# Attention block inputs in one 256 KB transfer, zero-padded V in the first batch, and a new table of ranks

## The chip, the core and the metric

The kernel runs on one core of a Trainium2 chip. The metric is the device time of one execution in microseconds (us); the kernel before has a median of 495.89 us over 3 runs. The engines are TensorE (PE, with its weight loads as PEld), VectorE (DVE), ScalarE (ACT), GpSimd (POOL) and SyncE (SP), which here only issues DMA transfers.

## The reference

Four batches, 8 heads, 768 tokens, 64 numbers a head. Each token attends to the first 8 tokens (global) and to itself and the 95 before it (local), with a distance bias per head. A gated MLP over the tokens follows.

```python
scores = q @ k.T / sqrt(64) - slope[h] * dist      # kept where global or local
a = softmax(scores)
x = (a @ v), heads side by side                    # [4, 768, 512]
h = relu(x @ w_in); u, v2 = h[..., :512], h[..., 512:]
vn = (v2 - mean(v2)) / sqrt(var(v2) + 1e-6)
out = (u * (w_spatial @ vn + b_spatial)) @ w_out   # w_spatial mixes the 768 tokens
```

## The kernel before

A batch is six blocks of 128 tokens, so there are 24 blocks, n = 0 to 23. For a block, `prep` (line 856) and `prep_v` (line 904) load q, k and v, `scores` (line 935) makes the probabilities and `values` (line 1003) multiplies them with V. A block's keys are its own 128 tokens and the 128 before it, whose first 32 rows are overwritten with the batch's global tokens; the block that opens a batch has its own 128 alone. So a block has 1 or 2 chunks of 128 keys.

The first batch (blocks 0 to 5) works in plain float32 (`whole_s`, `whole_v`), where a matrix product is two rows of the profile. From block 6 on, every operand is split into a high part `hi` and the rest `lo` (`hi_lo`, line 641), and the products are made of the parts. For that `prep` loads a block's q and k into `raw`, splits them (`split_qk`, line 887), and copies the parts by DMA into the layouts `q1`, `ql` and `kring` (`prep_k`, line 897): 18 transfers a block in all.

In `values` the probabilities of a pair of heads are transposed on PE, copied by ACT from a PSUM bank to `pth`, and multiplied with V into `ops`. In the first batch one product per pair and chunk multiplies 128 columns of V (two heads) with 256 columns of probabilities (both heads' tokens). Half of the result is wanted: head 0's rows under head 0's tokens and head 1's under head 1's. So two ACT copies of 64 rows each bring the halves together in a tile `c`, and from `c` the parts `xth` and `xtl` of x are made:

```python
ops[:, g % 2] = vring[:, chunk, g*128:(g+1)*128].T @ pth[:, chunk]   # [128, 256]
xs[0:64]   <- ops[0:64, :, 0:128]       # ACT, tile c
xs[64:128] <- ops[64:128, :, 128:256]   # ACT, tile c
xh <- xs ; xl <- xs - xh                # any engine
```

Meanwhile the weights are prepared. `w_in` and `w_out` arrive as 64-bit floats, in pieces of 512 KB into three `u` buffers, and `split_weights` (line 723) turns each into `hi` and `lo` with some ten instructions on DVE, ACT and POOL. The eight pieces of `w_in` end with eight DVE writes of `w_in_l`: the first four belong to the V half of the MLP (`mlp_v`, 128x512 products), the last four to the U half (`mlp_u`, products of `xth` and `xtl` with `w_in`, 128x256). `w_t` is the spatial matrix.

The order is not that of the code. All instructions are recorded, and `plan` (line 347) sorts them for all engines at once by a model of costs, with a rank for each step from the table `KEYS` (line 533). `keep_warm` then puts products with the identity matrix (`bank<-ident`), which nobody reads, into gaps that the plan foresees on PE. SP runs its list in order: a transfer that waits holds all behind it.

Of the kernel before, what the change touches and what calls it, by code (L numbers as in the profile page):

```python
# [10 lines left out]
F32 = mybir.dt.float32  # L11
# [15 lines left out]
CFG = {'WS': 6, 'WV': 6, 'kept': 'p', 'bias1': 'pppppppp', 'bias2': 'a', 'S': [['I01', 'A'], ['I00', 'T00', 'T01', 'A', 'V00', 'B00'], ['T02', 'T03', 'A', 'V01', 'U00'], ['T04', 'T05', 'A', 'V02'], ['Q00', 'Q01', 'A', 'V03', 'U01'], ['Q02', 'Q03', 'A', 'V04']], 'T': [['V15', 'U12', 'A'], ['G10', 'O10', 'A'], ['G11', 'O11', 'A'], ['G12', 'O12', 'V00', 'V01', 'U00', 'A'], ['V02', 'A'], ['V03', 'U01', 'A', 'V04']], 'END': ['V05', 'U02', 'G00', 'O00', 'G01', 'O01', 'G02', 'O02'], 'whi': 'aaax', 'wsub': 'xx', 'wadd': 'v', 'wth': 'a', 'wtl': 'p', 'vhi': 'p', 'vlo': 'p', 'qhi': 'xv', 'qlo': 'v', 'khi': 'a', 'klo': 'v', 'pth0': 'a', 'x0h': 'a', 'x0l': 'v', 'pth': 'a', 'xh': 'aa', 'c1': 'a', 'xl': 'vppv', 'vnh': 'xvpa', 'vnl': 'p', 'gm': 'x', 'gh': 'aa', 'gl': 'x', 'o': 'vava', 'norm0': 'p', 'norm': 'p', 'wp': 3, 'we': 'p', 'x0c': 1, 'xch': 'x', 'xcl': 'x', 'vrn': 'v', 'dup': 1, 'fold': '', 'xb': 1, 'div': 'v', 'rows': 'a', 'xf0h': 'aa', 'xf0l': 'pppp', 'xdiv': 'v', 'xbh': 'a', 'xbl': 'p', 'b_rawqk': 1, 'b_ev': 3, 'b_raw': 1, 'b_pr': 10, 'b_pth': 2, 'b_c1': 3, 'b_ps_s': 2, 'b_ps_p': 2, 'b_ps_o': 2, 'b_ps_m': 2}  # L27
# [195 lines left out]
def cost(op):  # L223

    out = op.writes[0]
    n = elements(out)
    src = op.reads[0] if op.reads else out
    psum = any(in_psum(x) for x in op.reads + op.writes[:1])
    parts = list(out.ap)[0][1]
    if op.eng == "tensor":  # L230
        if op.call == "transpose":
            return 109, 0, False
        n = elements(op.kw["rhs"])
        if op.kw["rhs"].dtype == F32:
            return 4 * max(n, 128) * .422, 0, False
        return {128: 111, 256: 120, 512: 229}[n], 0, False
    if op.eng == "sync":
        return 650, 330 + n * 4 * parts * .0024, False
# [298 lines left out]
def attn_then_spatial_gating_kernel(  # L537
# [23 lines left out]
    def cp(e, out, in_):  # L561
# [21 lines left out]

    B, NB, D, H, _ = q.shape
# [66 lines left out]

    def even(t):
        return t.rearrange("p (g two) x -> p two g x", two=2)[:, 0]

    def odd(t):
        return t.rearrange("p (g two) x -> p two g x", two=2)[:, 1]
# [66 lines left out]
    def split_weights(src, hi, lo, tag, x):  # L723
# [10 lines left out]
        if CFG["wp"] == 3:  # L734
# [7 lines left out]
            nc.vector.tensor_scalar(out=c, in0=m, scalar1=UPPER_MAX, scalar2=UPPER_MIN, op0=ALU.min, op1=ALU.max)  # L742
            nc.vector.tensor_scalar(out=ci, in0=ci, scalar1=4, scalar2=1, op0=ALU.logical_shift_left, op1=ALU.logical_shift_right)
            nc.vector.scalar_tensor_tensor(out=ci, in0=ci, scalar=0x40000000, in1=ai, op0=ALU.bitwise_xor, op1=ALU.bitwise_or)
            nc.vector.tensor_scalar(out=ai, in0=ci, scalar1=-0x800000, scalar2=None, op0=ALU.bitwise_and)
# [110 lines left out]
    def prep(n):  # L856
        b, i = divmod(n, NB)
        if whole_s(n):
            if n == 0:
                for x in range(2):  # L860
                    t = ring["q", x] = work.tile([P, H, P], F32, name="q0", tag=f"q{x}", bufs=1)
                    nc.gpsimd.memset(even(t)[64:128], 0.0)
                    nc.gpsimd.memset(odd(t)[0:64], 0.0)
# [503 lines left out]
```

## Time and profile before

| what | value |
|---|---|
| median of 3 runs | 495.89 us (495.59 to 496.63) |
| the profiled execution | 494.69 us |
| its span, first to last instruction | 492.9 us |
| PE busy | 472.0 us (96%), 3240 instructions |
| DVE, ACT, POOL busy | 357.2, 292.7, 273.0 us (72%, 59%, 55%) |
| mean busy share of the 16 DMA engines, queue q1 | 50.0% |
| mean granted TensorE clock | 0.994 |

The three times are those of the runs, the span is of one of them under the profiler; 1.8 us of that execution lie outside the span. PE's rows overlap, since a product starts before the one ahead has left the array: how long one takes is read from start to start in a dense stretch. Tile names stand without buffer numbers; `bank` is a PSUM bank, `ev` and `u` are scratch tiles of several uses.

### The profile page before, as it was taken

What the parts mean: (1) busy time and instruction counts of PE and PEld (TensorE: products, weight loads), DVE (VectorE), ACT (ScalarE), POOL (GpSimd) and SP (SyncE); (2) the same over time, 40 slices, a digit from 0 to 9 for tenths busy, and PEclk for the clock granted to TensorE, in tenths of its full rate; (3) what the DMA queues carried; (4) which work ended last, traced back from release to release, by engine and by line L of the source; (5) the groups of instructions that cost most, each with busy time, mean ns of one, the idle gap of its engine ahead of it and who ended that gap; (6) DMA issues with size and microseconds to landing.
All of it is one profiled execution on the core that took longest, in us unless ns stands there. A gap on an engine that the chain in (4) does not pass through costs nothing.

```text
span 492.9 us, 9972 instructions
## 1 busy us (share of the span) xinstructions
PE 472.0 (96%) x3240; PEld 430.8 (87%) x3240; DVE 357.2 (72%) x1014; ACT 292.7 (59%) x793; POOL 273.0 (55%) x429
## 2 busy tenths in 40 slices
PE   7988899999999999999999999999999999999995
PEld 7866597899999889898989999999988989999994
DVE  5789958785889788888868788787757598561532
ACT  3799789844754777676556566766733586520111
POOL 3689987777435564697565354794342565452000
PEclk9999999999999999999999999999998999999999
DMA  7995326237655767555573663766552671000012
GB/s 178 267 226 180 107 82 187 70 97 178 154 155 149 204 171 202 149 135 134 155 198 93 180 167 98 184 155 173 123 139 76 159 177 56 16 0 3 23 43 72
DMA packets 68269, 65.51 MB, mean 133 GB/s; under 512 B 6672, under 2 KB 49936, under 8 KB 68208
## 3 DMA queue, kind: packets, MB, share of 16 engines
q1 hardware_dynamic: 68208, 64.78, 50.0%
q8 instruction: 28, 0.46, 0.4%
q14 instruction: 33, 0.27, 0.2%
HBM read 29.76 MB, written 6.68 MB: 74 GB/s over the span
## 4 chain that ended last, share of the span: by engine, by line
PE 73%; ACT 7%; DMA 6%; DVE 4%; POOL 4%; SPq 3%; issue 2%; ACTq 0%; POOLq 0%
PE bank L39 64%; PE ops L39 8%; SPq L39 3%; ACT pr L39 3%; DMA raw<-in_k_dram 2%; DMA kring<-raw 2%; DVE bank L39 1%; POOL pr L39 1%; ACT ev L39 1%; DMA vring<-vg 1%; DMA q<-raw 1%; ACT pth L39 1%; ACT w_in_h L39 1%; ACT c L39 1%; POOL vring L39 1%
## 5 line engine op out<-in xcount | busy, mean ns | idle before, releaser
L39 POOL TENSOR_SCALAR pr<-pr,rc 128x256 f32<-128x256 f32 (+1 forms) x192 | 95.3, 513 | 41.7 <-DVE rc L39 24.8
L39 ACT ACTIVATE pr<-pr,mn 128x256 f32<-128x256 f32 (+1 forms) x192 | 92.0, 482 | 15.6 <-DVE mn L39 14.9
L39 DVE CUSTOM_DVE_ANT_0 pr<-bank,bias 128x256 f32<-128x256 f32 (+1 forms) x192 | 68.1, 396 | 19.0 <-PE bank L39 18.3
L39 DVE TENSOR_TENSOR c<-ops,c 64x256 f32<-64x256 f32 x144 | 60.5, 420 | 16.3 <-ACT c L39 13.0
L39 ACT ACTIVATE pth<-bank 128x512 fp32r<-128x512 f32 (+3 forms) x96 | 52.4, 558 | 31.1 <-PE bank L39 19.5
L39 PE MATMUL ops<-pth,vring 128*128 128x256 f32 x352 | 66.1, 313 | 4.3 <-ACT pth L39 1.7
L39 PE MATMUL bank<-kring,q 128*128 128x256 f32 (+1 forms) x384 | 66.9, 304 | 3.1 <-DVE w_in_l L39 1.4
L39 PE MATMUL bank<-ident,pr 128*128 128x128 f32 x352 | 60.6, 273 | 1.9 <-ACT pth L39 1.4
L39 PEld LDWEIGHTS ops<-pth,vring 128*128 128x128 f32 x352 | 51.8, 189 | 11.3 <-ACT c L39 3.5
L39 PEld LDWEIGHTS bank<-kring,q 128*128 128x128 f32 x384 | 55.0, 189 | 7.3 <-DVE w_in_l L39 1.8
L39 POOL TENSOR_TENSOR xtl<-c,xth 128x256 fp32r<-128x256 f32 x44 | 32.8, 747 | 50.7 <-ACT xth L39 47.3
L39 DVE TENSOR_TENSOR pth<-bank,pth 128x512 fp32r<-128x512 f32 (+1 forms) x72 | 45.5, 642 | 13.0 <-ACT pth L39 12.0
L39 PEld LDWEIGHTS bank<-ident,pr 128*128 128x128 f32 x352 | 43.3, 140 | 9.8 <-POOL pr L39 2.4
L39 PE MATMUL bank<-w_t_h,vnh 128*128 128x256 f32 x288 | 45.6, 285 | 1.1 <-ACT vnh L39 1.1
L39 PE MATMUL bank<-w_t_h,vnl 128*128 128x256 f32 x288 | 45.4, 284 | 0.0
L39 PE MATMUL bank<-w_t_l,vnh 128*128 128x256 f32 x288 | 45.0, 283 | 0.0
L39 ACT ACTIVATE c<-ops 64x256 f32<-64x256 f32 x96 | 36.3, 378 | 14.3 <-PE ops L39 12.2
L39 ACT ACTIVATE ev<-bank 128x512 f32<-128x512 f32 (+1 forms) x37 | 21.5, 585 | 37.1 <-PE bank L39 31.0
L39 PEld LDWEIGHTS bank<-w_t_h,vnh 128*128 128x128 f32 x288 | 38.6, 189 | 1.4 <-ACT vnh L39 1.3
L39 PEld LDWEIGHTS bank<-w_t_h,vnl 128*128 128x128 f32 x288 | 38.9, 189 | 0.3
L39 PEld LDWEIGHTS bank<-w_t_l,vnh 128*128 128x128 f32 x288 | 38.6, 189 | 0.1
L39 POOL TENSOR_TENSOR vnl<-ev,vnh 128x512 fp32r<-128x512 f32 x24 | 31.0, 1291 | 13.7 <-DVE vnh L39 5.3
(104 smaller groups left out, 983.4 us busy)
## 6 DMA issues: line engine op xcount, KB each, us to landing
q<-rawh SPq DMA_DIRECT2D x72, 128.0 KB, 2.4
q<-raw SPq DMA_DIRECT2D x72, 128.0 KB, 2.4
out_dram<-ev SPq DMA_DIRECT2D x23, 256.0 KB, 2.4
raw<-in_q_dram SPq DMA_DIRECT2D x36, 128.0 KB, 2.9
raw<-in_v_dram SPq DMA_DIRECT2D x18, 256.0 KB, 3.1
raw<-in_k_dram SPq DMA_DIRECT2D x36, 128.0 KB, 3.1
kring<-rawh SPq DMA_DIRECT2D x36, 128.0 KB, 2.6
kring<-raw SPq DMA_DIRECT2D x36, 128.0 KB, 2.6
```

The source lines that it names most:

```text
L39: getattr(self.real, self.call)(*[placed(x) for x in self.args], **{n: placed(x) for n, x in self.kw.items()})
```

## The change

1. On the host, q and k are laid out as [batch, block, head of the pair, 64, pair, 128 tokens], and v with the two heads of each pair exchanged.
2. The k of a block comes in one transfer of 128 partitions with 2 KB each, where two of 64 partitions with four runs of 512 bytes brought it. From block 6 on q does too. In the first batch q stays two transfers (the zeros between the heads have to stay), now with 2 KB a partition.
3. `kring` has a slot's heads next to each other, so that the copies into it write one run of 2 KB a partition.
4. In the first batch V is stored as zero, head 1, head 0, zero, head 1, head 0, ... (13 groups of 64 columns). A product per head, pair and chunk multiplies 128 columns of it, one head and zeros, with that head's 128 columns of probabilities, and all of a pair's products add up in one [128, 128] result. `xth` and `xtl` are made from it straight away: `xtl` by DVE alone, `xth` by ACT or DVE. The copies to `c` are gone there. A block's V lands in runs of 512 bytes instead of 2 KB, and POOL clears the zero columns once.
5. `KEYS` is another table, and the planner's costs of a small float32 product and of a transfer's issue are other ones. The order of all engines is anew.

Core of the diff (the key table, the general path for other sizes and a disused option are left out):

```diff
-            q1, kc = ring["q", n % 2], ring["k"][:, :, n % 3]
-            for half, dst in ((0, even(q1)), (1, odd(q1))):
-                s_ = slice(64 * half, 64 * half + 64)
-                nc.sync.dma_start(out=dst[s_], in_=q[b, i, :, half::2])
-                nc.sync.dma_start(out=kc[s_], in_=k[b, i, :, half::2])
+            q1 = ring["q", n % 2]
+            for j, s_ in enumerate(halves):
+                nc.sync.dma_start(out=q1[s_, j], in_=q[b, i, j])
+            nc.sync.dma_start(out=ring["k"][:, n % 3], in_=block(k, b, i))
...
+    def block(src, b, i):
+        return src[b, i].rearrange("two d g x -> (two d) g x")
...
         for i, cols in pieces:
-            for j, s_ in enumerate(halves):
-                nc.sync.dma_start(out=raw[s_, :, cols], in_=src[b, i, :, j::2, cols])
+            nc.sync.dma_start(out=raw[:, :, cols], in_=block(src, b, i)[:, :, cols])
...
-                ring["v", True] = work.tile([P, 3, DM], F32, name="vring0", tag="vring", bufs=1)
-            nc.sync.dma_start(out=ring["v", True][:, n % 3], in_=rows)
+                t = ring["v", True] = work.tile([P, 3, 3 * NP + 1, D], F32, name="vring0", tag="vring", bufs=1)
+                nc.gpsimd.memset(t[:, :, 0::3], 0.0)
+            nc.sync.dma_start(out=padded(n % 3, slice(0, P)), in_=rows)
...
-                for c in range(nch):
+                ops = opsring[:, n % 2].rearrange("p two x -> p (two x)").rearrange("p (g x) -> p g x", x=P)
+                for y in range(2 * nch):
+                    c, j = divmod(y, 2)
                     nc.tensor.matmul(
-                        ops[:, g % 2], lhsT=vring[:, order[c], g * P:(g + 1) * P], rhs=pth[:, c],
-                        start=(c == 0), stop=(c == nch - 1),
+                        ops[:, g], lhsT=vring[:, order[c], 3 * g + 2 - 2 * j:3 * g + 4 - 2 * j].rearrange("p x d -> p (x d)"), rhs=pth[:, c, j * P:(j + 1) * P],
+                        start=(y == 0), stop=(y == 2 * nch - 1),
                     )
                 if g % 2:
-                    for half, s_ in enumerate(halves):
-                        src = ops[s_, :, half * P:half * P + P]
-                            cp(E("x0h", half), xs[s_], src)
-                        hi_lo(xs, xh[:, gs, toks], xl[:, gs, toks], E("xch", g // 2), E("xcl", g // 2))
+                        hi_lo(ops[:, gs], xh[:, gs, toks], xl[:, gs, toks], E("x0h", g // 2), E("x0l", g // 2))
```

How the order moves, at three places. SP, the first transfers of the program, before (`q_0_100`, `kring_102`, `vring_116` are block 0's q, k and v, `q_0_101` block 1's q, the `u` tiles pieces of `w_in`):

```order
L39 DMA nraw<-in_n_global_dram 128x2
L39 DMA nraw<-in_n_local_dram 128x2
L39 DMA u_117<-in_moe_w_in_dram 128x1024
L39 DMA u_121<-in_moe_w_in_dram 128x1024
L39 DMA vring_116<-in_v_dram 128x512
L39 DMA q_0_100<-in_q_dram 64x4x128
L39 DMA kring_102<-in_k_dram 64x4x128
L39 DMA q_0_100<-in_q_dram 64x4x128
L39 DMA kring_102<-in_k_dram 64x4x128
L39 DMA u_119<-in_moe_w_in_dram 128x1024
```

and now:

```order
L39 DMA nraw<-in_n_global_dram 128x2
L39 DMA nraw<-in_n_local_dram 128x2
L39 DMA q_0_100<-in_q_dram 64x512 x2
L39 DMA kring_102<-in_k_dram 128x512
L39 DMA vring_116<-in_v_dram 128x4x128
L39 DMA u_117<-in_moe_w_in_dram 128x1024
L39 DMA u_121<-in_moe_w_in_dram 128x1024
L39 DMA u_119<-in_moe_w_in_dram 128x1024
L39 DMA b_bc<-in_moe_b_spatial_dram 128x768
L39 DMA q_0_101<-in_q_dram 64x512 x2
```

Block 0's q, k and v stand ahead of all pieces of `w_in` now, where two of these and V stood ahead of q and k.

PE, its first instructions, before (`bank<-kring` are the products of scores, `bank<-ident,pr` the transposes, `ops` the products with V):

```order
L39 MATMUL bank_85<-ident 128x128 x95
L39 MATMUL bank_85<-kring_102,q_0_100 128x128 x2
L39 MATMUL bank_86<-kring_102,q_0_100 128x128 x2
L39 MATMUL bank_87<-kring_102,q_0_100 128x128 x2
L39 MATMUL bank_88<-kring_102,q_0_100 128x128 x2
L39 MATMUL bank_89<-ident 128x128 x19
L39 MATMUL bank_89<-kring_102,q_0_101 128x256 x2
```

and now:

```order
L39 MATMUL bank_84<-ident 128x128 x55
L39 MATMUL bank_84<-kring_102,q_0_100 128x128 x2
L39 MATMUL bank_85<-kring_102,q_0_100 128x128 x2
L39 MATMUL bank_86<-kring_102,q_0_100 128x128 x2
L39 MATMUL bank_87<-kring_102,q_0_100 128x128 x2
L39 MATMUL bank_88<-ident 128x128 x27
L39 MATMUL bank_88<-ident,pr_108 128x128
L39 MATMUL bank_88<-ident,pr_109 128x128
L39 MATMUL bank_84<-ident,pr_110 128x128
L39 MATMUL bank_84<-ident,pr_111 128x128
L39 MATMUL ops_99<-pth_124,vring_116 128x128 x2
```

55 products with the identity stand ahead of block 0's scores instead of 95, and block 0's transposes and products with V come ahead of block 1's scores.

DVE, around the last write of `w_in_l`, before (`ISA pr` is a score, 128x256 for one head of a block):

```order
L39 ISA pr_110,mn_106<-bank_86,bias 128x256
L39 ISA mn_106 128x1
L39 TENSOR_TENSOR w_in_l<-bank_85,ev_104 128x512
L39 ISA pr_111,mn_106<-bank_86,bias 128x256
L39 ISA mn_106 128x1
L39 BN_STATS st_142<-ev_103 128x6
L39 CAST xth_140<-c_2_134 128x2x128
```

and now, from the last but two on:

```order
L39 TENSOR_TENSOR w_in_l<-bank_86,ev_104 128x512
L39 SCALAR_TENSOR_TENSOR bank_89<-bank_89,raw_0_118 128x512
L39 CAST xth_137<-ops_99 128x2x128
L39 TENSOR_SCALAR raw_0_118<-bank_89 128x512
L39 TENSOR_SCALAR bank_86<-ev_104 128x512
L39 TENSOR_TENSOR xtl_138<-ops_99,xth_137 128x2x128
L39 TENSOR_SCALAR bank_86<-bank_86 128x512
L39 TENSOR_TENSOR bank_89<-bank_89,w_in_h 128x512
```

The making of x (`xth`, `xtl` from `ops`) now stands between the steps of the weights on DVE, and the last write of `w_in_l` has 34 scores of 128x256 ahead of it instead of 25, 8 `xtl` instead of none and 3 `xth` instead of none.

## Rows read from the trace of the kernel before

**Rows 1.** Busy time by stretches; us, then each engine, granted clock, DMA share, GB/s.
```profile
0.00:15.50 15.50, 12.46 (x101) 12.46 (x102) 7.20 (x40) 4.33 (x11) 7.50 (x23) 1.00 0.80 188
15.50:60.65 45.15, 38.43 (x197) 29.21 (x196) 42.12 (x131) 39.79 (x112) 37.71 (x54) 1.00 0.73 197
15.50:38.50 23.00, 20.04 (x115) 15.56 (x113) 21.23 (x72) 21.37 (x65) 16.89 (x29) 1.00 0.93 234
60.65:487.70 427.05, 421.08 (x2946) 389.08 (x2945) 307.92 (x844) 248.24 (x670) 227.78 (x353) 1.00 0.47 125
370.70:374.80 4.10, 4.07 (x11) 3.20 (x12) 3.94 (x8) 0.29 (x1) 0.00 (x0) 0.58 0.19 68
450.00:493.00 43.00, 37.69 (x262) 34.80 (x260) 14.26 (x21) 5.65 (x10) 0.00 (x0) 0.97 0.11 40
```

**Rows 2.** Timeline of PE in the opening; start us, us, instruction, count.
```profile
3.04 12.02 PE L39 MATMUL bank<-ident 128*128 128x128 f32 x95 [3.04 <-POOL ident masks.py:199]
14.90 1.95 PE L39 MATMUL bank<-kring,q 128*128 128x128 f32 x16
16.68 2.24 PE L39 MATMUL bank<-ident 128*128 128x128 f32 x19
61.15 0.82 PE L39 MATMUL bank<-xth,w_in_h 128*128 128x256 f32 x4
```

**Rows 3.** Timeline of PE in dense stretches, for the time of one product.
```profile
67.08 1.04 PE L39 MATMUL bank<-ident,pr 128*128 128x128 f32 x8
67.96 1.03 PE L39 MATMUL bank<-kring,q 128*128 128x256 f32 x4
68.82 1.89 PE L39 MATMUL ops<-pth,vring 128*128 128x256 f32 x8
...
310.25 1.10 PE L39 MATMUL bank<-w_in_h,xth 128*128 128x512 f32 x4
311.19 1.10 PE L39 MATMUL bank<-w_in_l,xth 128*128 128x512 f32 x4
```

**Rows 4.** Timeline of DVE: first score, last write of w_in_l, a score.
```profile
15.55 0.29 DVE L39 CUSTOM_DVE_ANT_0 pr<-bank,bias 128x128 f32<-128x128 f32 x1 [2.63 <-PE bank L39]
...
59.96 0.69 DVE L39 TENSOR_TENSOR w_in_l<-bank,ev 128x512 fp32r<-128x512 f32 x1
60.56 0.41 DVE L39 CUSTOM_DVE_ANT_0 pr<-bank,bias 128x256 f32<-128x256 f32 x1
```

**Rows 5.** Timeline of SP: the first transfers of size.
```profile
1.64 0.90 SPq L39 DMA_DIRECT2D u<-in_moe_w_in_dram  x2
```

**Rows 6.** DMA issues; transfers, KB each, median us from issue to landing.
```profile
q<-in_q_dram SPq DMA_DIRECT2D x12, 128.0 KB, 7.2
```

**Rows 7.** Groups of 0 to 110 us, and one of the page; busy, mean ns, idle before.
```profile
L39 ACT ACTIVATE c<-ops 64x256 f32<-64x256 f32 x24 | 9.0, 377 | 2.8 <-PE ops L39 2.5
L39 DVE CAST xth<-c 128x256 fp32r<-128x256 f32 x2 | 0.8, 404 | 0.8 <-ACT c L39 0.8
L39 DVE TENSOR_TENSOR c<-ops,c 64x256 f32<-64x256 f32 x144 | 60.5, 420 | 16.3 <-ACT c L39 13.0
```

**Rows 8.** SP's issues into `raw`; duration ns min/median/max, first and last start.
```profile
L39 SPq DMA_DIRECT2D raw<-in_k_dram x36: 533/568/620, 101.6 to 394.5; - x36
L39 SPq DMA_DIRECT2D raw<-in_v_dram x18: 332/544/599, 19.1 to 379.1; - x18
```

**Rows 9.** Who PE waited for from 60 us on; us in total, times, longest.
```profile
PE bank L39 <- DVE ev L39: 2.0, 1, 2.0
PE bank L39 <- DMA kring<-raw: 1.1, 1, 1.1
```

**Rows 10.** Chain of waits ahead of two stalls of PE; start us, us, what.
```profile
332.00 3.52 DMA kring<-raw
335.59 3.44 DMA raw<-in_k_dram
...
365.64 2.81 DMA raw<-in_k_dram
```

More of the change, by code (lines that the diff above doesn't have):

```diff
@@ L234, in cost @@
         if op.kw["rhs"].dtype == F32:
-            return 4 * max(n, 128) * .422, 0, False
+            return max(234, 4 * n * .422), 0, False
         return {128: 111, 256: 120, 512: 229}[n], 0, False
     if op.eng == "sync":
-        return 650, 330 + n * 4 * parts * .0024, False
+        run = n // list(out.ap)[-1][1] * parts
+        return (520 if run <= P and parts == P else 650 if run <= 256 else 1250), 330 + n * 4 * parts * .0024, False
     if op.eng == "scalar":
@@ L581, in nb @@
         return CFG["b_" + key]
-    B, NB, D, H, _ = q.shape
+    B, NB, _, D, _, _ = q.shape
+    H = 2 * q.shape[4]
     S = NB * P
@@ L650, in two @@
             e.tensor_tensor(**kw)
[L652 to L656, printed above, removed]
     def setup_bias():
@@ L860, in prep @@
                 for x in range(2):
[L861 to L869 removed]
+                    t = ring["q", x] = work.tile([P, 2, NP, P], F32, name="q0", tag=f"q{x}", bufs=1)
+                    for j, s_ in enumerate(halves):
+                        nc.gpsimd.memset(t[halves[1 - j], j], 0.0)
+                ring["k"] = work.tile([P, 3, NP, P], F32, name="kring0", tag="kring", bufs=1)
+            q1 = ring["q", n % 2]
+            for j, s_ in enumerate(halves):
+                nc.sync.dma_start(out=q1[s_, j], in_=q[b, i, j])
+            nc.sync.dma_start(out=ring["k"][:, n % 3], in_=block(k, b, i))
             return q1, None
         if n == CFG["WS"]:
[L872 removed]
+            ring["k"] = work.tile([P, 2, 2, NP, P], F32R, name="kring", tag="kring", bufs=1)
             if i:
@@ L882, in prep @@
         prep_k(n, [(i, slice(0, P))])
-        return q1.rearrange("p two g x -> p g two x"), ql.rearrange("p two g x -> p g two x")
+        return q1, ql
     halves = [slice(64 * j, 64 * j + 64) for j in range(2)]
+    def block(src, b, i):
+        return src[b, i].rearrange("two d g x -> (two d) g x")
     def split_qk(x, src, b, pieces):
@@ L897, in prep_k @@
     def prep_k(n, pieces):
-        kc = ring["k"].rearrange("p (g two) s x -> p two g s x", two=2)[:, :, :, n % 2]
+        kc = ring["k"][:, n % 2]
         parts = split_qk(1, k, n // NB, pieces)
@@ L920, in prep_v, with padded @@
             nc.sync.dma_start(out=vg[b], in_=vr[0:NGMAX].bitcast(F32).rearrange("p g x d -> p (g x d)"))
+    def padded(slot, part):
+        return ring["v", True][part, slot, 0:3 * NP].rearrange("p (g x) d -> p g x d", x=3)[:, :, 1:3]
     def split_v(n, pieces):
@@ L927, in split_v @@
         raw = raw.rearrange("p (g two d) -> p g two d", two=2, d=D)
-        hi_lo(raw, vr[:, :, 0::3], vr[:, :, 1:3], E("vhi"), E("vlo"))
+        hi_lo(raw, vr[:, :, 1:3], vr[:, :, 0::3], E("vhi"), E("vlo"))
     xt = {}
@@ L941, in scores, with globs @@
         kept = kg[:, 0:NP] if whole_s(n) else kg
+        def globs(x):
+            if whole_s(n):
+                return kring[:, x, :, 0:NGMAX]
+            return kring[:, x].rearrange("p j g x -> p (j g) x")[:, :, 0:NGMAX].bitcast(F32)
         if i == 0:
-            copy(kept, kring[:, :, cur, 0:NGMAX] if whole_s(n) else kring[:, :, cur, 0:NGMAX].bitcast(F32))
+            copy(kept, globs(cur))
             sl = slice(cur, cur + 1)
@@ L946, in scores @@
             if n == CFG["WS"]:
-                copy(kept, kring[:, :, prev, 0:NGMAX].bitcast(F32))
+                copy(kept, globs(prev))
             sl = slice(min(cur, prev), max(cur, prev) + 1, abs(cur - prev))
@@ L961, in scores @@
                 if whole_s(n):
-                    nc.tensor.matmul(sp[:, j], lhsT=q1[:, h], rhs=kring[:, g, sl], start=True, stop=True)
+                    nc.tensor.matmul(sp[:, j], lhsT=q1[:, j, g], rhs=kring[:, sl, g], start=True, stop=True)
                     continue
                 for y, a in enumerate((q1, ql)):
-                    nc.tensor.matmul(sp[:, j], lhsT=a[:, g, j], rhs=kring[:, h, sl], start=(y == 0), stop=(y == 1))
+                    nc.tensor.matmul(sp[:, j], lhsT=a[:, j, g], rhs=kring[:, sl, j, g], start=(y == 0), stop=(y == 1))
             for j in range(2):
@@ L999, in scores @@
         if 1 <= i < NB - 1:
-            copy(kring[:, :, cur, 0:NGMAX], kept)
+            copy(globs(cur) if whole_s(n) else globs(cur).bitcast(F32R), kept)
         yield
@@ L1065, in values @@
                     nc.tensor.matmul(
-                        ops[:, j], lhsT=vring[:, order[c], g, 2 * j:2 * j + 2].rearrange("p x d -> p (x d)"),
+                        ops[:, j], lhsT=vring[:, order[c], g, 2 - 2 * j:4 - 2 * j].rearrange("p x d -> p (x d)"),
                         rhs=pth[:, 2 * c + j].rearrange("p x y -> p (x y)"), start=(c == 0), stop=(c == nch - 1),
@@ L1093, in values @@
             if whole_v(n):
-                nc.sync.dma_start(out=vring[0:NGMAX, n % 3], in_=v[b, 0:NGMAX, :])
+                nc.sync.dma_start(out=padded(n % 3, slice(0, NGMAX)), in_=v[b, 0:NGMAX, :])
             else:
@@ L1262, in general @@
                 for j in range(NB):
-                    for half in range(2):
-                        nc.sync.dma_start(out=kt[64 * half:64 * half + 64, :, j * P:(j + 1) * P], in_=k[b, j, :, half::2])
+                    nc.sync.dma_start(out=kt[:, :, j * P:(j + 1) * P], in_=k[b, j].rearrange("two d g x -> (two d) g x"))
                 for i in range(NB):
                     rq = work.tile([P, NP, P], F32, name="grq")
-                    for half in range(2):
-                        nc.sync.dma_start(out=rq[64 * half:64 * half + 64], in_=q[b, i, :, half::2])
+                    nc.sync.dma_start(out=rq, in_=q[b, i].rearrange("two d g x -> (two d) g x"))
                     qt = work.tile([P, NP, P], F32, name="gqt")
@@ L1344 @@
             n, h, t, d = a.shape
-            a = a.reshape(n, h, t // P, P, d).transpose(0, 2, 4, 1, 3)
+            a = a.reshape(n, h // 2, 2, t // P, P, d).transpose(0, 3, 2, 5, 1, 4)
         elif name == "v":
-            a = a.transpose(0, 2, 1, 3).reshape(a.shape[0], a.shape[2], -1)
+            n, h, t, d = a.shape
+            a = a.reshape(n, h // 2, 2, t, d)[:, :, ::-1].transpose(0, 3, 1, 2, 4).reshape(n, t, -1)
         elif name == "moe_w_spatial":
```

31 lines of the change are left out of this document (13 added, 18 removed).

## The prediction, made before the run

> **What bounds the kernel now.** I read the busy times by stretches first, then PE's timeline, then who PE waited for. From 60.65 us on PE is busy 421.08 of 427.05 us at full granted clock [rows 1]: products stand end to end, and nothing that another engine does there is worth anything unless it ends one of the 6.0 us of waits. Before that it is otherwise. PE runs 95 products with the identity until 14.90 us, 19 more at 16.68, and the first product of the MLP's U half starts at 61.15 [rows 2]. In the order, PE has until then 40 transposes, 8 scores of 128x128, 27 of 128x256, 20 products with V and 24 MLP products of 128x512. From start to start a transpose takes 0.110 us, a float32 product of 256 columns, two rows of the profile, 0.430, an MLP product 0.235 [rows 3], a float32 product of 128 columns 0.223 (16 rows in 1.78 us [rows 2]). The sum is 4.4 + 1.8 + 11.6 + 8.6 + 5.6 = 32.0 us. So at 61.15 us PE is **29.1 us behind** a PE that never waited, and of that lag nothing comes back later. The opening is where time can be won.
>
> What holds the opening is DVE: from its first score at 15.55 to the end of the last `w_in_l` at 60.65 [rows 4] it is busy 42.12 of 45.15 us, 93%, with ACT at 88% and POOL at 84% [rows 1]. The U products start right behind that write.
>
> **The change, part by part.** The opening. Block 0's q, k and v stand first on SP, and 55 products with the identity stand ahead of the scores. 95 took 11.86 us [rows 2], so 55 take 6.9 us from 3.04 on: scores at 9.9 us. The first transfer of size issues at 1.64 us, and two issues take 0.90 us [rows 5], so k, the third, issues at 2.5; with the 7.2 us from issue to landing [rows 6], of a time when two pieces of `w_in` were ahead, it is there by 9.7. DVE's first score, 0.65 us behind PE's as before [rows 2, 4], comes at 10.6 us instead of 15.55.
>
> From there DVE's work decides. By the order it has to do more before the last `w_in_l`: 9 scores of 128x256 at 0.41 [rows 4], 3.7 us; 8 `xtl` out of PSUM, for which the nearest row is the PSUM sum of 64x256 at 0.420 [rows 7], 3.4 us; 3 `xth` at 0.404 [rows 7], 1.2 us; the small instructions around them I put at 2.7 us. That is 11.0 us on 49.3 (7.20 and 42.12 [rows 1]), 60.3 in all, of which some 3.7 stand ahead of the first score, since half of the 7.20 us of bias and weight steps has moved behind it. Left are 56.6 us. At 93% busy they end at 10.6 + 60.9 = 71.5 us; at POOL's 84% at 78.0; at 95% at 70.2. I take 90%, between DVE's and ACT's share, since more on PE now hangs on ACT too: 73.5 us.
>
> But PE does more before it has to wait for that write: 72 transposes, 8 and 37 scores, 64 products with V of 128 columns and 44 MLP products, 7.9 + 1.8 + 15.9 + 14.3 + 10.3 = 50.2 us, and eight U products at half of 0.235, 1.0 us: 51.2. The lag is then 73.5 - 51.2 = 22.3 us: **6.8 us won**, with ends of 2.3 (84%) and 10.1 (95%).
>
> PE's own work. 44 products of 0.430 become 88 of 0.223: 18.9 to 19.6 us, **0.7 us lost**, all of it on the path. The two pieces of `kring` with a larger step between them cost nothing: block 3's two slots lie apart before already, and its products take what the others take.
>
> ACT loses 24 copies at 377 ns, 9.0 us [rows 7]; POOL loses the `xtl` that it made from `c` and gains the clearing of V's zero columns, once. Both are hidden behind DVE; should DVE be faster than I think, ACT is late next.
>
> SP. From block 6 on a block has 16 transfers instead of 18: four issues into `raw` at 0.57 us become two. For 128 runs of 2 KB the row of V's transfers bounds the price, 0.33 to 0.60 [rows 8]; SP saves 1.1 to 1.6 us a block. In the first batch k goes from 12 issues to 6, but V's come in 512 runs, for which no row stands. It costs between 0.33 (128 runs) and 1.04 us (from 0.33 for 128 and 0.57 for 256 runs [rows 8], drawn on); I take the upper end. Of these only block 0's V stands ahead of something that is waited for, the pieces of `w_in`, which are issued 2.7 us later in all. DVE covers that with block 0's scores; without that cover it costs those 2.7 us, which the end at 84% holds.
>
> What SP is worth later: two of PE's longest stalls, 2.0 us and 1.1 us [rows 9], lie at the end of chains through `raw<-in_k` and the copies into `kring`, from 332 and from 366 us on [rows 10]. Behind the second the clock is at 0.58 for 4.10 us [rows 1], a mean between its two levels of 1.2 and 2.4 GHz, after PE had stood still for 2.0 us; that costs 4.10 x 0.42 = 1.7 us. Together 4.8 us. The ranks move these places, so I take half, **2.4 us won**. All 4.8 is one end; the other is a loss of 3.7, a new stall as long as the longest now, with its slow clock.
>
> Sum, against the profiled execution's own 494.69 us: 6.8 + 2.4 - 0.7 = 8.5 us less, 486.2. The median of the runs is 1.2 us above that execution, so **487.4 us** for the median.
>
> **The size of the pieces.** While PE writes out only, with 2 KB rows, the DMA engines move 40 GB/s at a share of 0.11, 364 GB/s at full share; in 15.5 to 38.5 us, with mostly 512-byte pieces, 234 at 0.93, 252 GB/s [rows 1]. In the first batch 3.1 MB of q and k change to 2 KB pieces and 1.6 MB of V to 512 bytes; 1.5 MB by 1/252 - 1/364 makes 1.8 us of DMA time less. I leave it out of the sum and put it at the lower end of the range. The Trainium skill, "DMA: Bandwidth & Descriptors", section "Specifications", has 512 bytes as enough for line rate, so that by it larger pieces would win nothing; the rows of this trace speak against it.
>
> **Rivals.** *A, the opening waits for data.* For it: the DMA engines are 93% busy in 15.5 to 38.5 us [rows 1], the bytes are the same, and `w_in` comes later. Against it: DVE is just as busy in that stretch, and has work of an arrived piece to do. Then the opening wins the 1.8 us alone and nothing is won later: 495.89 - 1.8 + 0.7 = 494.8 us. If larger pieces move no faster, the 1.8 us fall away too: 496.6 us. That is what the rule of the Trainium skill just cited would make of it.
>
> *B, DVE is overloaded, and the kernel is slower.* The place is the last `w_in_l`; the point, its end at 80.3 us (51.2 + 29.1): 56.6 us of work in 69.7, 81% busy. Below that the change loses, since `xtl` must now be made by DVE, which reads PSUM, and every wait for ACT's `xth` stands in DVE's queue ahead of the weights. At 75% the write ends at 86.1 us, 5.8 us worse, and the time is 495.89 + 5.8 + 0.7 = 502.4. For it: three `xth` and eight `xtl` between the weight steps. Against it: before, DVE got to 92% and 93% with the same chains [rows 1].
>
> *C, the later blocks take part of it back.* The new ranks make a stall of 3.7 us where two of the old ones go: -6.8 + 3.7 + 0.7, 493.5 us. For it: 18 blocks are ordered anew by a model. Against it: SP has more room.
>
> **Numbers.** About 0.2% is what a measurement can tell from no change here, 1 us. Forecast 0.68; A 0.12, two thirds of it with faster large pieces; B 0.08; C 0.12. Faster: forecast, C, and a third of A, whose 494.8 us lie at the bound, 0.84; same: the rest of A, 0.08; slower: B, 0.08. The lower end is -10.1 - 4.8 - 1.8 + 0.7 = -16.0, 479.9 us, taken as 480.0. Upward the range takes in C with 1 us and leaves out B and most of A: 494.5. The forecast alone lies between 483 and 491.
>
> **What would show it.** Right: PE's first score at about 10 us; DVE's last `w_in_l` at 70 to 77 us with the U products right behind; PE busy from there on with under 6 us of waits; 64-row copies only from block 6 on. Wrong: U products starting later than 80 us, or as many DMA waits of PE as now.

## The result, and the profile after

The change takes **488.22 us** (median of 4 runs, 487.03 to 490.76), the kernel before in the same comparison 496.01 (495.59 to 496.63): 0.9849 of it, interval 0.9819 to 0.9878. The prediction was 487.4, between 480.0 and 494.5. The profiled execution of the change took 489.19 us, 5.5 less than that of before, its span 487.4 against 492.9. In the medians the gain is 7.8 us, 2.3 more than between these two executions. The forecast was right in sign and size, but two of its terms were not, and they missed in opposite directions.

Busy time of the change by stretches: us, each engine (instructions), granted clock, DMA share, GB/s. They answer to [rows 1], with the cuts at DVE's first score and at the end of the last `w_in_l`.

```profile
0.00:11.90 11.90, 8.86 (x61) 8.86 (x62) 3.48 (x23) 1.99 (x4) 4.91 (x15) 1.00 0.65 208
11.90:70.74 58.84, 55.84 (x360) 48.24 (x360) 53.44 (x184) 51.38 (x147) 50.49 (x78) 1.00 0.67 197
...
70.74:487.40 416.66, 401.09 (x2869) 372.85 (x2868) 298.81 (x815) 232.22 (x624) 211.98 (x327) 1.00 0.46 123
```

The timeline of PE in the opening, as [rows 2].

```profile
3.04 8.39 PE L39 MATMUL bank<-ident 128*128 128x128 f32 x55 [3.04 <-POOL ident masks.py:199]
11.27 1.95 PE L39 MATMUL bank<-kring,q 128*128 128x128 f32 x16
...
70.26 0.83 PE L39 MATMUL bank<-xth,w_in_h 128*128 128x256 f32 x4
```

The timeline of DVE, as [rows 4]: the first score and the last write of `w_in_l`.

```profile
11.92 0.29 DVE L39 CUSTOM_DVE_ANT_0 pr<-bank,bias 128x128 f32<-128x128 f32 x1 [3.88 <-PE bank L39]
...
70.05 0.69 DVE L39 TENSOR_TENSOR w_in_l<-bank,ev 128x512 fp32r<-128x512 f32 x1
```

DVE is busy 53.44 of 58.84 us from its first score on, 91%, and the last `w_in_l` ends at 70.74, among the first U products, as before. PE's first U product stands at 70.26 us and has, by the counts and prices of the prediction, 50.2 us of work ahead of it: a lag of 20.1 us where it was 29.1. **The opening won 9.0 us, not 6.8.** From 60 to 70 us PE is busy for all 10.00 us, so the lag comes from waits further ahead, not from one wait for that last write.

For all runs below one measure serves: over PE's records, the time from the start of one to the start of the next, less the price of its shape [rows 3] (0.119 us for a row of 256 columns of the split parts, the median of such rows). Summed up to the first U product, with the identity products counted as waiting, this is the lag (29.1 before, 20.0 after); summed from there on, it is what PE loses later.

Later losses are 9.7 us before and 13.2 in the profiled execution of the change. From 70.74 to 482.50 us, where PE's last product is, it is busy 400.79 of 411.76 us: 11.0 us of waits, where a stretch that ends as far before the end had 6.0 before [rows 1]. Who PE waited for from 70 us on in the change (us in total, times, longest), as [rows 9]:

```profile
PE ops L39 <- DVE c L39: 2.4, 3, 2.1
PE bank L39 <- DMA kring<-raw: 2.1, 2, 1.6
PE bank L39 <- POOL pr L39: 1.9, 3, 0.9
PE bank L39 <- DVE mn L39: 1.4, 3, 0.5
...
PE ops L39 <- DMA vring<-vg: 0.5, 1, 0.5
```

So -9.1, +3.5, +0.7 for PE's own work and -0.6 behind PE's last product make the measured -5.5 us.

SP's issues into `raw` (duration ns min/median/max, first and last start), as [rows 8]; then landings of the DMA groups, us from issue, as [rows 6]:

```profile
L39 SPq DMA_DIRECT2D raw<-in_q_dram x18: 333/339/529, 16.0 to 386.1; - x18
L39 SPq DMA_DIRECT2D raw<-in_v_dram x18: 328/372/587, 18.3 to 385.7; - x18
L39 SPq DMA_DIRECT2D raw<-in_k_dram x18: 328/334/1083, 87.3 to 387.1; - x18
```
```profile
q<-in_q_dram SPq DMA_DIRECT2D x12, 128.0 KB, 4.7
...
raw<-in_k_dram SPq DMA_DIRECT2D x18, 256.0 KB, 2.8
```

Per block SP issues q and k in 2 x 0.335 instead of 4 x 0.57 us: 1.6 us less, the upper end of what was said. A q of the first batch lands after 4.7 us instead of 7.2.

### The profile page after: what moved, and what is told of

Its sections match the earlier page's. It is cut to its first block, busy times and chain, and to the rows that moved or that the text cites. A ratio compares the mean times of both kernels' runs of the same rounds, so it can differ in the third digit from the quotient of the medians.

```text
span 487.4 us, 10076 instructions
## 1 busy us (share of the span) xinstructions
PE 465.8 (96%) x3286; PEld 430.0 (88%) x3286; DVE 355.7 (73%) x1021; ACT 285.6 (59%) x773; POOL 267.4 (55%) x419
## 4 chain that ended last, share of the span: by engine, by line
PE 60%; DMA 12%; DVE 10%; ACT 8%; issue 4%; SPq 3%; POOL 2%; DVEq 0%; ACTq 0%; POOLq 0%
PE bank L39 54%; PE ops L39 6%; ACT pr L39 4%; SPq L39 3%; DMA kring<-raw 3%; DVE pr L39 2%; DVE c L39 2%; DMA q<-raw 2%; DMA kring<-in_k_dram 2%; DMA raw<-in_k_dram 2%; DMA gl<-in_moe_w_spatial_dram 1%; DMA raw<-in_q_dram 1%; DVE bank L39 1%; ACT pth L39 1%; DMA gh<-in_moe_w_spatial_dram 1%
## 5 line engine op out<-in xcount | busy, mean ns | idle before, releaser
L39 POOL TENSOR_SCALAR pr<-pr,rc 128x256 f32<-128x256 f32 (+1 forms) x192 | 93.3, 504 | 27.4 <-DVE rc L39 13.9
L39 PE MATMUL bank<-kring,q 128*128 128x256 f32 (+1 forms) x384 | 65.2, 304 | 6.2 <-DMA kring<-raw 2.1
L39 PE MATMUL ops<-pth,vring 128*128 128x256 f32 (+1 forms) x440 | 63.2, 282 | 3.9 <-DVE c L39 2.4
L39 ACT ACTIVATE pth<-bank 128x512 fp32r<-128x512 f32 (+3 forms) x96 | 51.4, 556 | 24.7 <-PE bank L39 16.8
L39 PEld LDWEIGHTS ops<-pth,vring 128*128 128x128 f32 x440 | 57.3, 190 | 8.0 <-ACT pth L39 2.7
L39 POOL TENSOR_TENSOR xtl<-c,xth 128x256 fp32r<-128x256 f32 x36 | 28.5, 793 | 53.9 <-ACT xth L39 44.9
L39 PEld LDWEIGHTS bank<-ident,pr 128*128 128x128 f32 x352 | 42.3, 140 | 9.4 <-POOL pr L39 5.0
L39 PE MATMUL bank<-w_t_l,vnh 128*128 128x256 f32 x288 | 46.6, 286 | 0.0
L39 ACT ACTIVATE rawh<-raw 128x512 fp32r<-128x512 f32 x29 | 18.3, 630 | 37.0 <-DMA raw<-in_k_dram 21.5
L39 ACT ACTIVATE gh<-ev 128x512 fp32r<-128x512 f32 x24 | 15.1, 629 | 37.0 <-DVE ev L39 18.2
```

The costliest lines, as they stand in the source:

```text
L39: getattr(self.real, self.call)(*[placed(x) for x in self.args], **{n: placed(x) for n, x in self.kw.items()})
```

## The experiments

### What holds the opening: runs in a fixed order

These keep the order of all engines to the instruction, but for what is named.

**Work added to DVE.** Each of its eight writes of `w_in_l` is done twice.

```diff
         for op in warm:
             op.issue()
+            if op.eng == "vector" and op.writes[0].tensor.name == w_in_l[:].tensor.name:
+                op.issue()
```

> The change with each of DVE's eight writes of w_in_l done twice, in place; the order is the same otherwise. 8 x 0.68 us make 5.4 us more of DVE's work ahead of the first U product. Theory 'DVE bounds the opening': the last w_in_l 5.0 to 5.8 us later (75.5 to 76.5 us), and the time 4.5 to 6 us above 488.2: 492.7 to 494.2 us. Rival 'the opening waits for data or for ACT': it moves by under 1.5 us, 488 to 490 us.

Measured: 493.10 us (491.24 to 493.81), ratio 0.9940 (0.9912 to 0.9967), 4.9 above the change. In DVE's timeline the last pair is

```profile
73.20 1.41 DVE L39 TENSOR_TENSOR w_in_l<-bank,ev 128x512 fp32r<-128x512 f32 x2
```

It ends at 74.62 instead of 70.74, 3.9 us later for 5.8 us of added work (a pair takes 1.41 where one took 0.69, eight times); the rest went into waits that DVE had (its wait for ACT's `pr` fell from 1.9 to 0.7 us). The end comes earlier than expected, the median time is as expected, and the rival of hidden work falls. Between the profiled executions the time grew by 2.3 us: the lag by 3.1 (to 23.1), while the later losses fell to 12.3. DVE bounds the opening, with about 2 us of slack.

**An earlier start for DVE.** 24 products with the identity stand ahead of the first scores instead of 55.

```diff
-    out, last = [], WARM_FROM
+    out, last, count = [], WARM_FROM, 0
...
-                    out.extend(make(bank) for _ in range(int((gap - 300) // 112)))
+                    count += 1
+                    out.extend(make(bank) for _ in range({1: 24}.get(count, int((gap - 300) // 112))))
```

> The change with 24 instead of 55 products with the identity ahead of block 0's scores, and every other instruction in the same order. In the change k has landed by 6.5 us and DVE has its first bias ready at 8.0, yet the first score comes at 11.27, behind those products. Theory 'DVE bounds the opening': the first score at 8.2 us, DVE's first at 8.9, the last w_in_l 2.5 to 3.2 us earlier than 70.7, and the time 2 to 3 us below the change's 488.2: 485 to 486 us. Rival 'the opening waits for pieces of w_in': the last w_in_l moves by under 1 us, 487.4 to 488.4 us. Rival 'taken back later': the opening is 3 us shorter, but the waits after 70 us grow by as much; 487.5 to 489 us.

Measured: **483.98 us** (483.57 to 486.12), ratio 0.9771 (0.9737 to 0.9805), apart from the change's interval. PE's and DVE's timelines:

```profile
3.05 5.38 PE L39 MATMUL bank<-ident 128*128 128x128 f32 x24 [3.05 <-POOL ident masks.py:199]
8.22 2.37 PE L39 MATMUL bank<-kring,q 128*128 128x128 f32 x16
```
```profile
9.29 0.29 DVE L39 CUSTOM_DVE_ANT_0 pr<-bank,bias 128x128 f32<-128x128 f32 x1 [1.18 <-PE bank L39]
...
67.67 0.69 DVE L39 TENSOR_TENSOR w_in_l<-bank,ev 128x512 fp32r<-128x512 f32 x1
```

DVE starts 2.63 us earlier and ends 2.38 us earlier: the opening passes on nine tenths of it. The time fell by 4.2, more than expected; losses after the first U product are 10.0 us in this execution instead of 13.2. They did not grow, as one rival had it.

**How far this goes**, together with the halved transfers that are tried below (the edit there and this one in one kernel).

> The change with 24 products with the identity and with the 256 KB transfers of q and k issued as two of 64 partitions each. Each alone gave 484.0 and 486.3 us. If what they win is apart (2.4 us of the opening by the products, shorter waits through raw and kring by the halves): 481.5 to 483.5 us. If the halves' 2 us were only the spread of the change's own times (487.0 to 490.8): 483.5 to 485 us.

Measured: 484.25 us (481.32 to 485.10), ratio 0.9745 (0.9712 to 0.9778); not to be told from 24 products alone. The same with 16:

```diff
-                    out.extend(make(bank) for _ in range({1: 24}.get(count, int((gap - 300) // 112))))
+                    out.extend(make(bank) for _ in range({1: 16}.get(count, int((gap - 300) // 112))))
```

> As ident_24_halves with 16 products. They end at 6.5 us, when k lands; DVE has its first bias ready at 8.1, so its first score comes at 8.2 instead of 9.3. Theory 'DVE bounds the opening': another 0.8 to 1.2 us less than with 24. Rival 'the slow clock of the first products reaches into the scores and transposes': PE at the lower level until after 9 us, and nothing won, within 0.5 us of ident_24_halves.

Measured: 485.17 us (483.35 to 486.76), ratio 0.9759 (0.9726 to 0.9792). In the profiled executions DVE did start at 8.04 us instead of 8.30, but the last `w_in_l` ended at 71.16 instead of 67.88. PE's timeline, and its clock by stretches (us, PE busy, clock, DMA share, GB/s):

```profile
15.36 0.33 PE L39 MATMUL bank<-ident,pr 128*128 128x128 f32 x1 [1.53 <-POOL pr L39]
...
18.11 3.75 PE L39 MATMUL bank<-kring,q 128*128 128x256 f32 x8 [1.38 <-DMA kring<-in_k_dram]
```
```profile
12.00:16.00 4.00, 2.41 (x14) 1.00 1.06 264
16.00:18.00 2.00, 0.71 (x5) 0.76 0.65 173
18.00:20.00 2.00, 1.90 (x5) 0.50 0.85 230
20.00:22.00 2.00, 2.00 (x7) 0.50 1.05 217
22.00:24.00 2.00, 2.00 (x10) 0.54 1.01 328
```

PE came so early that it stood still for 1.53 us for POOL's `pr` and 1.38 us for a transfer of k, and the clock fell from 2.4 to 1.2 GHz from about 17 to 24 us. So in this execution a start a quarter of a microsecond earlier ended 3.3 us later. Neither of the two expected ways is right there: the low level did not reach on from the start, it came back. But this is the slowest of six executions (486.76 us, mean granted clock 0.989). The other five have 0.995 to 0.998, too high for a fall as long as this one, which alone takes 0.007 off the mean, and took 483.35 to 485.85 us, where the six with 24 took 481.32 to 485.10. So with 16 nothing more is won; that it loses by such a fall is shown for one execution alone.

**The same in the kernel before**, with 75 products instead of 95.

```diff
-                    out.extend(make(bank) for _ in range(int((gap - 300) // 112)))
+                    count += 1
+                    out.extend(make(bank) for _ in range({1: 75}.get(count, int((gap - 300) // 112))))
```

> The kernel before with 75 instead of 95 products with the identity ahead of block 0's scores, the order the same otherwise. There k has landed at 12.8 us and the scores start at 14.90, so at most 2.1 us of the opening are these products. Theory 'the order of the first transfers sets the start, and DVE the rest': the first score at 12.8 us, the last w_in_l 1.5 to 2.1 us earlier, 493.7 to 494.6 us against 495.8. Rival 'the products alone held the opening of before, and the change won by having fewer': it wins 4 us or more, 492 us or less. Rival 'data holds the opening of before': under 0.7 us.

Measured: 494.18 us (492.50 to 495.16), ratio 0.9943 (0.9920 to 0.9966). The first score came at 12.66 us, as expected when k lands, and the last `w_in_l` ended at 58.96 instead of 60.65: 1.7 of the 2.2 us arrived. Identity products were no more than this part of the opening of before; the rest of the change's gain is its order and its structure.

### Larger pieces, or fewer transfers?

Both runs keep the change's order. In the first q and k have a gap behind every 512 bytes in DRAM, so number and size of the transfers stay and the pieces are as before. In the second the pieces stay at 2 KB and each 256 KB transfer goes out as two.

```diff
             a = a.reshape(n, h // 2, 2, t // P, P, d).transpose(0, 3, 2, 5, 1, 4)
+            a = _np.concatenate([a, a[..., 0:16]], axis=-1)
...
+    q, k = q[..., 0:P], k[..., 0:P]
     B, NB, _, D, _, _ = q.shape
```

> The change with a gap of 64 bytes behind every 512 bytes of q and k in DRAM, so that their transfers keep their number, size and order but consist of 512-byte pieces as before. Theory 'larger pieces are worth little here': 1.8 us of DMA time in the opening, hidden behind DVE, and issues into raw at 0.57 to 1.1 instead of 0.335 us, which show in PE's waits for kring by under 1.5 us; 488 to 490 us. Rival 'the larger pieces carry the change': the first score or the last w_in_l comes 2 us later or more, or the later waits through raw grow by 3 us: 491.5 us or more.

```diff
         for op in warm:
+            x = op.kw.get("in_")
+            if op.eng == "sync" and x.tensor.name in (q.tensor.name, k.tensor.name) and list(op.kw["out"].ap)[0][1] == P:
+                for s_ in halves:
+                    y = Op()
+                    y.call, y.args, y.real, y.kw = op.call, (), op.real, {n: placed(z)[s_] for n, z in op.kw.items()}
+                    y.issue()
+                continue
             op.issue()
```

> The change with every 256 KB transfer of q or k issued as two of 64 partitions, the pieces still 2 KB and the order the same otherwise. SP gets 6 issues more in the first batch and about 2 more a block later, 0.33 to 0.6 us each. Theory 'SP's issues are hidden': 487.5 to 489.5 us, PE's waits for kring<-raw at most 1.5 us above the change's 2.1. Rival 'fewer issues carry the change': the later waits through raw and kring grow by 3 us or more, 491 us or more.

Measured: 512-byte pieces 497.91 us (495.46 to 504.01), ratio 1.0045 (1.0017 to 1.0073); halves 486.28 (485.44 to 487.32), ratio 0.9811 (0.9786 to 0.9835). **In this order the size of the pieces matters, the number of transfers does not.** With small pieces all of the gain is gone; with halves nothing is lost, perhaps something is won (the intervals of halves and change overlap). This does not say that large pieces are what the change won by: the order was made for them, and the kernel before, with 512-byte pieces and an order of its own, loses only 9.7 us in the later blocks. An order made for small pieces was not tried with this structure. The small pieces also begin 576 bytes apart here, and whether that costs something was not tried apart.

Where it goes is the surprise. The opening with 512-byte pieces is not longer: lag 18.5 against 20.0, last `w_in_l` at 69.22. The losses after it are 22.3 us against 13.2. SP's issues and then the landings of that run:

```profile
L39 SPq DMA_DIRECT2D raw<-in_q_dram x18: 590/592/799, 15.8 to 393.7; - x18
...
L39 SPq DMA_DIRECT2D raw<-in_k_dram x18: 568/590/593, 85.8 to 395.1; - x18
```
```profile
raw<-in_q_dram SPq DMA_DIRECT2D x18, 256.0 KB, 3.5
...
raw<-in_k_dram SPq DMA_DIRECT2D x18, 256.0 KB, 3.2
```

An issue takes 0.59 instead of 0.335 us, and the landing, counted from the start of the issue, comes 0.4 to 0.5 us later, twice a block. PE's five longest stalls stand where the change has one too, and are longer; some of the change's smaller ones shrink or are gone. One of the five, in the change and then with 512-byte pieces, from PE's timelines:

```profile
238.00 0.44 PE L39 MATMUL bank<-ident,pr 128*128 128x128 f32 x2 [0.93 <-POOL pr L39]
```
```profile
241.57 0.44 PE L39 MATMUL bank<-ident,pr 128*128 128x128 f32 x2 [2.03 <-POOL pr L39]
```

Behind four such stalls the clock falls, which the change's own execution does not show ahead of its last products; two of them (us, engines, clock, DMA share, GB/s):

```profile
236.00:246.00 10.00, 7.97 (x55) 7.77 (x55) 7.26 (x23) 6.96 (x22) 5.05 (x9) 0.83 0.73 177
364.30:374.00 9.70, 7.35 (x38) 6.61 (x38) 6.38 (x27) 6.16 (x21) 6.56 (x11) 0.82 0.64 148
```

The granted clock is at 0.50 for 13.6 us in all behind these four, and of the 9.1 us more of later losses 6.0 lie there. Yet an execution of the same kernel at a mean clock of 0.998 took 495.86 us, so the slow clock is not the whole of it.

The issue and landing of the raw loads do not by themselves explain the stalls either. The run with halves, its issues and landings:

```profile
L39 SPq DMA_DIRECT2D raw<-in_q_dram x36: 476/532/1887, 18.1 to 382.3; - x36
L39 SPq DMA_DIRECT2D raw<-in_k_dram x36: 465/489/1478, 87.4 to 384.2; - x36
```
```profile
raw<-in_q_dram SPq DMA_DIRECT2D x36, 128.0 KB, 2.7
raw<-in_k_dram SPq DMA_DIRECT2D x36, 128.0 KB, 2.6
```

There SP spends 2.0 us a block on these issues, where it spends 1.2 with 512-byte pieces. From the first issue of a block's q to its last landing it takes 4.2 us with halves, 3.5 with 512-byte pieces and 3.0 in the change (k: 3.6, 3.2 and 2.8; medians of 18 blocks). So the halves lengthen this chain more than the small pieces do, and lose nothing. What the small pieces lengthen that the halves do not stays open. One row points the right way: the copies `kring<-rawh` land after 3.1 us with small pieces, 2.9 in the change and 2.4 with halves. Whether that is it was not tried.

### Ranks and structure

Four runs change what the ranks were fitted to, and the order with it. In the first two the tables are exchanged between the kernels.

```diff
-KEYS = {'start': -188.6341, ('P', 0): -32.8668,
...
+KEYS = {'start': -148.4611, ('P', 0): -89.9124,
...
```

> The kernel before with the ranks of the change alone (old layout, V not padded, ACT's copies kept). Theory 'order': the opening is won by the order, block 0's q, k and v ahead of w_in and more work packed on DVE; then PE's first score comes at 12 to 13 us (58 products with the identity ahead of it, and two more issues of SP than in the change), the lag of PE at the first U product falls from 29 to 20 to 23 us, and the time is 487 to 491 us. Theory 'structure': without the larger transfers and the padded V the new order does not keep DVE supplied; the lag stays above 26 us and the time is 493 to 499 us.

> The changed kernel with the ranks of before. Theory 'order': scores start at 14 to 15.5 us again behind 92 products with the identity, the lag at the first U product is 27 to 30 us, and the time is 494 to 498 us. Theory 'structure': larger transfers and the 24 copies that ACT loses win by themselves; lag below 25 us, 488 to 492 us.

The other two take one half of the structure back, with the change's ranks: V's layout, products and copies, or q's and k's layout and transfers (there with the planner's costs of before as well).

```diff
-                for y in range(2 * nch):
+                if g % 2 == 0:
+                    ops = opsring[:, g // 2]
+                for c in range(nch):
...
-                        ops[:, g], lhsT=vring[:, order[c], 3 * g + 2 - 2 * j:3 * g + 4 - 2 * j].rearrange("p x d -> p (x d)"), rhs=pth[:, c, j * P:(j + 1) * P],
+                        ops[:, g % 2], lhsT=vring[:, order[c], g * P:(g + 1) * P], rhs=pth[:, c],
```

> The change with V as before (not padded, 44 products of 256 columns, ACT's copies of the halves back), the ranks of the change kept. The padded V alone is then what is missing. Theory 'order': the lag at the first U product is within 2 us of the change's 20, PE has 0.7 us less work, and the time is 486 to 491 us. Theory 'structure, by V': ACT's 9.0 us of copies come back ahead of the w_in pieces and DVE waits for them; lag 23 us or more, 491 to 496 us.

```diff
-            nc.sync.dma_start(out=ring["k"][:, n % 3], in_=block(k, b, i))
+            for half, dst in ((0, even(q1)), (1, odd(q1))):
...
+                nc.sync.dma_start(out=kc[s_], in_=k[b, i, :, half::2])
...
-            nc.sync.dma_start(out=raw[:, :, cols], in_=block(src, b, i)[:, :, cols])
+            for j, s_ in enumerate(halves):
+                nc.sync.dma_start(out=raw[s_, :, cols], in_=src[b, i, :, j::2, cols])
```

> The change with q and k as before (512-byte runs, four transfers a block in the first batch, four issues into raw instead of two), V padded and the ranks of the change kept. Theory 'order': the first score 1 us later, the lag 20 to 23 us, later stalls as in the change, 487 to 492 us. Theory 'structure, by q and k': the transfers come 2 us or more later all through the opening, lag 23 us or more, and the stalls through raw and kring from block 6 on grow past the change's 2.1 us; 491 to 497 us.

A fifth gives the change the ranks of before from block 6 on (here one entry of them).

```diff
-('P', 6): 12.1657,
+('P', 6): 26.274,
```

> The change with its own ranks for the first batch's weights and blocks 0 to 5, and the ranks of before for everything later. Theory 'the opening is won by the first ranks with the new structure, and ranks of another structure cost in the later blocks': the lag at the first U product is 20 to 22 us as in the change, and PE's losses after it grow from 13 to 20 us or more; 494 to 506 us. Rival 'ranks matter in the opening only': losses after it within 3 us of the change's, 486 to 491 us.

| kernel | us | ratio, interval | first score | lag | later losses |
|---|---|---|---|---|---|
| before | 496.01 | 1 | 14.90 | 29.1 | 9.7 |
| the change | 488.22 | 0.9849 (0.9819 to 0.9878) | 11.27 | 20.0 | 13.2 |
| before, ranks of the change | 500.97 | 1.0108 (1.0076 to 1.0141) | 12.03 | 25.9 | 21.8 |
| change, ranks of before | 514.87 | 1.0390 (1.0354 to 1.0425) | 16.33 | 28.1 | 33.0 |
| change, V as before | 522.34 | 1.0536 (1.0462 to 1.0611) | 10.79 | 30.5 | 34.3 |
| change, q and k as before | 504.93 | 1.0217 (1.0171 to 1.0264) | 11.41 | 22.1 | 25.5 |
| change, late ranks of before | 510.38 | 1.0268 (1.0223 to 1.0313) | 10.71 | 24.4 | 29.6 |

All five are slower than the kernel before, and all five expectations missed the time, "structure" and "order" alike. The first score follows the ranks; but neither new ranks nor new structure wins the opening alone: of the 29.1 us of lag the ranks leave 25.9, the structure 28.1. Under the change's ranks the padded V is the larger part of the lag: q and k as before leave it at 22.1, V as before at 30.5, where PE waits 2.4 us for ACT's `pth` and 1.4 us for ACT's copies `c` between 10 and 72 us. And a table of ranks that was made for another structure costs 9 to 21 us more in the later blocks than the change's 13.2. The fifth run shows the size: only later ranks differ in it, and its later losses are 29.6 us (its lag grew too, by over 4). Where they go, by PE's waits from 73 us on in that run:

```profile
PE ops L39 <- DVE c L39: 3.6, 2, 2.3
PE bank L39 <- DVE mn L39: 2.7, 4, 1.0
PE bank L39 <- POOL pr L39: 2.6, 3, 1.7
PE bank L39 <- ACT xth L39: 1.5, 1, 1.5
```

No one engine or queue stands out. Since these runs mix a fitted with an unfitted table, they don't price the parts of the structure: what V's layout is worth with ranks of its own was not tried.

## Why the prediction was right

The mechanism of the opening was right. That the sum came within 1 us of the median is luck in part: against the profiled execution the opening gave 2.2 us more than was said, and the later blocks lost 3.5 where 2.4 were to be won.

**What bounds the opening: right.** DVE does, as both fixed-order runs show: a later end for more work, an earlier one for an earlier start. Rival A, the opening waiting for data, falls with them, and with the 512-byte pieces, which left the opening as long as it was. Rival B, DVE overloaded, did not come: 91% busy, the last `w_in_l` at 70.74 where the point was 80.3.

**The start of the scores: 1.4 us late.** The step that failed is "95 took 11.86 us, so 55 take 6.9". They took 8.2: the first 21 stand 0.213 us apart and the rest 0.110. In before the first 14 did, so a mean over 95 hid it; other executions have 13 to 28. The spacing doubled is what 1.2 instead of 2.4 GHz would make of it, but the granted clock reads 1.00 over the whole stretch, so only the spacing shows it, and that it is the clock is argued. The Trainium skill, "TensorE: Matmul & The Clock Gate", section "Part 1: The HAM clock gate (the "warmup" mystery)", says that this number changes with the run and not to "fit to a specific cold count"; the runs agree.

**The opening: 9.0 us instead of 6.8.** The term was mis-sized in DVE's work and pace. From its first score to the last `w_in_l` it is busy 53.44 us, where 56.6 were said, at 91% where 90% was taken; 3.48 us lie ahead, as said (3.7). So it had 7.6 us more to do than before (56.92 on 49.32), not 11.0. One cause can be read in DVE's timeline:

```profile
69.35 0.42 DVE L39 CUSTOM_DVE_ANT_0 pr<-bank,bias 128x256 f32<-128x256 f32 x1
...
69.70 0.42 DVE L39 CUSTOM_DVE_ANT_0 pr<-bank,bias 128x256 f32<-128x256 f32 x1
```

Durations overlap: a score lasts 0.42 us and the next starts after 0.35. Priced from start to start, as the prediction did for PE and not for DVE, its 20 added instructions of this size cost some 1.4 us less. The rest was not traced. The end at 70.74 lies within the 70 to 77 us that were to show it.

**PE's own work: right, but at the low end.** 16 rows of V products start 1.89 us apart in the change, with the step to the next group, 0.236 us a product in place of 0.223; 88 of them make at most 1.2 us more than the 0.7 said; the median over all of them is 0.224, so the rest are waits.

```profile
28.55 2.05 PE L39 MATMUL ops<-pth,vring 128*128 128x128 f32 x16
30.44 1.04 PE L39 MATMUL bank<-ident,pr 128*128 128x128 f32 x8
```

**SP relief: the step that failed.** "I take half, 2.4 us won" came out as a loss of 3.5 in the profiled execution. SP was relieved as said, and the two stalls went, with the slow clock behind one. But the new order has others: 12 of over half a microsecond after the first U product where there were 5. This is rival C's direction, at nearly its price in this execution, though in many small stalls and not in one. Two of the forecast's own signs went against it here: "under 6 us of waits" became 11.0, and PE's waits for DMA, which were to be fewer, are three of 2.6 us in all, where before had three of 2.0 (1.1 [rows 9], and two for `vring<-vg` of 0.9 in all); one of the three is of 1.56 us for `kring<-raw`, at 117.21. One execution is not the whole, though. With 2 KB pieces and the same order the later losses are 7.4 to 13.2 us in the profiled executions of six kernels, so against before's 9.7 the term lies between a gain of 2.3 and a loss of 3.5, within the ends that were given; and if the opening and PE's own work are alike in all executions, the medians' 7.8 us leave it a loss of about 1.

**The size of the pieces: dismissed in the wrong place.** The 1.8 us were put to the opening's DMA time and left out. The rate did rise there. From 15 to 38 us, before, the change, and the change with 512-byte pieces:

```profile
15.00:38.00 23.00, 20.04 (x116) 15.62 (x115) 20.73 (x70) 20.87 (x63) 16.91 (x29) 1.00 0.95 238
```
```profile
15.00:38.00 23.00, 20.79 (x130) 17.37 (x129) 21.99 (x73) 21.35 (x65) 19.21 (x39) 1.00 0.72 223
```
```profile
15.00:38.00 23.00, 20.77 (x129) 17.22 (x127) 21.99 (x72) 21.35 (x63) 19.53 (x39) 1.00 0.86 227
```

At full share that is 251, 310 and 264 GB/s. It buys nothing, since DVE is the bound. The pieces matter in the later blocks, and there 512-byte pieces cost 9.7 us in this order. The prediction had put only SP's issue time there; by the run with halves that is not what costs, and the cause is open. The Trainium skill's rule that 512 bytes are enough for line rate ("DMA: Bandwidth & Descriptors", "Specifications") does not hold in these rows: the same order moves 15% less per DMA time with them. Their start every 576 bytes is a rival here; against it stands that before, without such gaps, moves no more, 251 GB/s.

## What to carry to other kernels

Ask of every wait ahead of the engine that bounds a stretch whether its length was planned or needed: here 31 warm-up products held DVE back for 2.6 us with the data already landed, and taking them out gave half as much again as the change; taking out eight more gave nothing further. In an order made for 2 KB pieces, 512-byte pieces cost 9.7 us with the DMA engines half idle (48.9% busy), and splitting a transfer in two cost nothing, though it lengthened issue and landing: a longer transfer is not by itself a longer kernel. A fitted order belongs to one structure: change the structure under it, or the table alone, and the later losses grow by 9 to 21 us, so such runs do not price the parts of a change; and a part that is priced in a fixed order is priced for that order alone.

The best version run is the change with 24 products, 483.98 us (with the halves 484.25, the same): 0.977 of before.

## What the runs showed of the hardware

In each run 13 to 28 products at the start stood 0.213 us apart before they stood 0.110 apart, at a granted clock that reads 1.00. After stand-stills of 1.53 and 1.38 us close together the granted clock was at 0.50, 1.2 GHz, for some 7 us; after one of 2.03 us in the run with 512-byte pieces it fell too, after one of 2.10 us in the change it did not. The median issue on SP took 0.335 us for a 256 KB transfer of 2 KB pieces and 0.59 for one of 512-byte pieces; two halves with 64 partitions took 0.49 to 0.53 each. V's transfers of the first batch, with 512-byte runs, were issued in 0.60 us (median of ten, four of them smaller ones), not in the 1.04 that the prediction had drawn on.
